# Products of the identity by itself in TensorE's early holes

## The chip, the cores and the metric

One core of one Trainium2 chip runs the whole program as one launch. The metric is the device time in microseconds (us). Five engines are named below: TensorE (PE, with its weight loads as PEld), VectorE (DVE), ScalarE (ACT), GpSimd (POOL) and SyncE (SP), which issues the DMAs.

## The reference

Three blocks follow one another, all in float32:

```python
scores = scale * q @ k.T                                   # 4 batches, 8 heads, 576 x 576, head size 64
scores = where(scores >= max(scores) - tau, scores, -1e9)  # tau = 0.02
attn = exp(scores - max) / (sum + 1e-9);  x = attn @ v     # -> 2304 x 512
g = relu(x @ w_in) ** 2;  y = g @ w_out                    # 512 -> 2048 -> 512
logits = y @ phi                                           # 32 slots: 8 experts of 4
slots = softmax(logits over tokens).T @ y
slots = relu(slots @ w1[e]) @ w2[e]                        # per expert, 512 -> 1024 -> 512
out = softmax(logits over slots) @ slots                   # 2304 x 512
```

## The kernel before, in words

**Front.** `setup()` builds an identity matrix: GpSimd writes it, VectorE copies it to `ident_r` (L280), and `ident` is the same memory read as float32. SyncE then loads five chunks of w_in (128 x 512, `c_load`, L328), the first kt and qt (L536), and goes on with chunks, v, and the kt and qt of later pairs of heads. VectorE and, for every second chunk, ScalarE rework each chunk (`c_low` L344, `c_scale` L338 or L340, the joining `c_shift` L348). For each four chunks TensorE multiplies parts of them by themselves into one PSUM tile (`gram`, `w_gram`, L412: four products a chunk), VectorE takes the diagonal (`w_diag`, L415), TensorE sums it over the partitions (`gtotal`, `w_sum`, L421), and VectorE makes a power-of-two scale from it (`w_scale`, L304 to L306). With that scale ScalarE writes the high half of each chunk (`w_hi`, L437), and the low half is made by VectorE (`w_lo`, L440), by GpSimd (L445, L450) or by TensorE with ScalarE (`w_diff`, L454 and L455).

**Attention.** A tile is 128 queries of a pair of heads. TensorE makes its scores (`s`, L694 and L699) in the only PSUM buffer of that kind. VectorE scales each head and takes its row bound (`top`, L738); when both heads are done, the scores of the next tile may be written. ScalarE takes the exponential (`expo`, L750), VectorE zeroes what lies under the threshold and sums (`keep`, L754), TensorE transposes (`turn`, L275), ScalarE moves the result out of PSUM (`p_evac`, L821), and TensorE multiplies by v. The squares of v are summed for a scale (`v_abs` on ScalarE L559 and L560, `v_sum` on TensorE L564, `v_scale` on VectorE L569).

**The feed-forward block and the end.** From about 140 us on, products of 256 tokens by w_in (L1233), by w_out's precomputed logits, and their transposes run between the attention tiles. The expert block follows from 566 us on: its weights come by DMA while TensorE multiplies them.

**The order.** All of it up to the expert block is put in order by `Plan` while the program is built. Each operation has an engine, a cost, dependencies and a key. The planner keeps a clock of its own and starts on each free engine the ready operation of the lowest key; the order in which it starts them is the order of the instructions on each engine, and nothing on the chip changes it. `HOP` (0.17) is what it adds from one engine to another, `DMA_LEAD` (1.13) and `DMA_TAIL` (0.95) what it adds to a DMA, which holds its model of the bus for 1.46 per chunk and 0.95 per kt or qt. Costs that matter here, in its microseconds: `c_low` 0.35, `c_shift` 0.61, `c_scale` 1.255 on ScalarE and 0.7 on VectorE, `w_gram` 1.1, `s` 1.4, `w_sum` 0.3, `top` 0.813, `v_sum` 0.25, `turn` 0.49, `w_scale` 0.6. TensorE's small results share the tag "mm": four PSUM buffers (`MMB`), taken in rotation, so that the fifth user waits until the first has given its buffer back. A buffer is given back 0.17 after its last reader ends.

Of the kernel before, what the change touches and what calls it, by code (L numbers as in the profile page):

```python
# [36 lines left out]
class Plan:  # L37
# [4 lines left out]
    def __init__(self, caps, shared, wait, ahead):  # L42
        self.shared, self.ops, self.queue = shared, [], {}
        self.caps, self.wait, self.now, self.pending = dict(caps), wait, 0.0, 0
        self.free = {e: 0.0 for e in ENGINES}
        self.cand = {e: [] for e in ENGINES}
        self.gen, self.taken, self.given = {}, {}, {}
        self.times = []
        self.bus, self.ahead = 0.0, ahead
        self.port = 0.0  # L50

    def add(self, eng, cost, fn, deps=(), key=0.0, acq=(), rel=(), dma=0.0, port=False):
# [40 lines left out]
    def start(self, o):  # L93
# [22 lines left out]
        for u in o.users:  # L116
            u.left -= 1
            u.ready = max(u.ready, self.seen(o, u))
            if not u.left:
                self.cand[u.eng].append(u)  # L120

    def run(self, goal=None):
        goal = goal and list(goal)
        if not self.queue:
            for o in sorted(self.ops, key=lambda o: o.key):
                for tag in o.acq:
                    self.queue.setdefault(tag, []).append(o)
        while self.pending:
            if goal is not None:
                goal = [o for o in goal if o.end is None]  # L130
                if not goal:
                    return
            for e in ENGINES:
                if e == "SP" and self.bus - self.now > self.ahead + 1e-6:
                    continue
                if self.free[e] <= self.now + 1e-6:
                    ok = [o for o in self.cand[e] if o.ready <= self.now + self.wait and self.fits(o)]
                    best = min(ok, key=lambda o: o.key, default=None)
                    if best is not None and best.ready <= self.now + 1e-6:
                        self.start(best)  # L140
            while self.times and self.times[0] <= self.now + 1e-6:
                heapq.heappop(self.times)
            assert self.times, "the plan is stuck"
            self.now = heapq.heappop(self.times)
# [3 lines left out]
def tile_kernel(  # L148
# [13 lines left out]
    nc = tc.nc  # L162
# [4 lines left out]
    E, _, F = w1.shape  # L167
    NP = H // 2
    KC = DM // 128
# [44 lines left out]
    QF = 10  # L214
    HDV = (0, 2)
    XHA = ()
    QL = 19.2
    LL = 16.0

# [7 lines left out]
    plan = Plan(  # L227
        dict(
            s=1, ma=1, mm=MMB, old=4, u=UB, e=EB, pt=PTB, rp=3, rb=2, rr=2, hl=HB, vh=1, mx=2, xp=XPB, xh=2, xl=1, gt=MC // 2 + 1,
            gk=GB, l4=1, dT=1, qt=QKB, kt=QKB, vraw=2, vbd=2,  # L230
            sm=5, raw64=RB, cv=CB,
        ),
        ("mm", "ma", "xp", "old"),
        WAIT,
        DQ,
# [6 lines left out]
    def mm_tile(tag="mm"):  # L242
        return psp[tag].tile([128, 512], F32, tag=tag, name="mm")
# [5 lines left out]
    ident = ident_r.bitcast(F32)  # L249
# [27 lines left out]
    def setup():  # L277
        make_identity(nc, sg[:, 0:128])
        nc.vector.memset(ones, 1.0)
        nc.vector.tensor_copy(ident_r, sg[:, 0:128])  # L280
        nc.vector.tensor_scalar(minus, ident, -1.0, None, ALU.mult)
        nc.sync.dma_start(out=tau_sb, in_=tau.partition_broadcast(128))
        nc.vector.tensor_scalar(tau_p, tau_sb, 0.0, None, ALU.max)
        nc.vector.tensor_scalar(nscale, tau_sb, 0.0, -SCALE, ALU.is_ge, ALU.mult)
        nc.vector.tensor_reduce(stack_i, ident.rearrange("p (g s) -> p s g", s=NS), AX.X, ALU.add)
        for g in range(1, NG):
            nc.vector.tensor_copy(stack_f[:, NS * g:NS * g + NS], stack_i)
# [22 lines left out]
    def conv_ops():  # L310
# [82 lines left out]
        def weight_parts(f4):  # L393
            four = range(KC * f4, KC * f4 + KC)
            s2, t, f, inv = [wsc[:, i, f4:f4 + 1] for i in range(4)]
            ws = {}

            def total():
                ws["p"] = mm_tile()
                nc.tensor.matmul(ws["p"][:, 0:KC], ones.to_broadcast([128, 128]), wst[:, four[0]:four[0] + KC], start=True, stop=True)  # L400

            def wscale():
                nc.vector.tensor_reduce(s2, ws["p"][:, 0:KC], AX.X, ALU.add)
                power(s2, t, f, inv)

            def gram():
                ws["g"] = mm_tile()
                for i, n in enumerate(four):
                    y = squared[n][0]["p"].bitcast(BF16)
                    for c in range(0, CW, 128):  # L410
                        z = y[:, 2 * c + 1:2 * c + 256:2]
                        nc.tensor.matmul(ws["g"][:, 0:128], z, z, start=i == 0 and c == 0, stop=i == KC - 1 and c == CW - 128)  # L412

            def diag():
                nc.vector.scalar_tensor_tensor(  # L415
                    ws["g"][:, 0:128], ws["g"][:, 0:128], 1.0, ident, ALU.mult, ALU.mult, accum_out=wst[:, f4:f4 + 1]
                )

            def gtotal():
                ws["p"] = mm_tile()  # L420
                nc.tensor.matmul(ws["p"][:, 0:1], ones.to_broadcast([128, 128]), wst[:, f4:f4 + 1], start=True, stop=True)  # L421

            k = C0 + (four[0] + KC) * TC
            deps = [squared[n][4] for n in four]
            if GRAM:
                gg = add("w_gram", "PE", 1.1, gram, deps, k, ["mm"])
                deps = [add("w_diag", "DVE", 0.3, diag, deps + [gg], k, rel=[("mm", gg)])]
            tt = add("w_sum", "PE", 0.3, gtotal if GRAM else total, deps, k, ["mm"])
            w = add("w_scale", "DVE", 1.0, (lambda: power(ws["p"][:, 0:1], t, f, inv)) if GRAM else wscale, [tt], k, rel=[("mm", tt)])
            wscaled.append(w)  # L430
            scaled = sg[:, f4 * 128:(f4 + 1) * 128]
            wi = add("w_id", "POOL", 0.35, lambda: nc.gpsimd.tensor_scalar(scaled, ident, f, None, ALU.mult), [w], k)
            for n in four:
                o, hi, lo, a, _ = squared[n]

                def high(o=o, hi=hi):
                    nc.scalar.activation(hi, o["p"], AF.Copy, scale=f)  # L437

                def low(o=o, hi=hi, lo=lo):
                    nc.vector.scalar_tensor_tensor(lo, o["p"], f, hi, ALU.mult, ALU.subtract)  # L440

                def times(o=o):
                    for c in range(0, CW, CW // PIECES):
                        i = slice(c, c + CW // PIECES)
                        nc.gpsimd.tensor_tensor(o["p"][:, i], o["p"][:, i], f.to_broadcast([128, CW // PIECES]), ALU.mult)  # L445

                def rest(o=o, hi=hi, lo=lo):
                    for c in range(0, CW, CW // PIECES):
                        i = slice(c, c + CW // PIECES)
                        nc.gpsimd.tensor_tensor(lo[:, i], o["p"][:, i], hi[:, i], ALU.subtract)  # L450

                def diff(o=o, hi=hi):
                    o["pt"] = mm_tile()
                    nc.tensor.matmul(o["pt"], minus, hi, start=True, stop=False)  # L454
                    nc.tensor.matmul(o["pt"], scaled, o["p"], start=False, stop=True)  # L455

                def round_(o=o, lo=lo, n=n):
                    if n % 8 in DIFD:
                        nc.vector.tensor_copy(lo, o["pt"])
                    else:  # L460
                        nc.scalar.activation(lo, o["pt"], AF.Copy)

                k += TC / 4
                h = add("w_hi", "ACT", 0.6, high, [w], k)
                if n % 8 in DIFF:
                    m = add("w_diff", "PE", 1.1, diff, [h, wi], k, ["mm"], [("gt", a)])
                    conv_in.append(add("w_round", "DVE" if n % 8 in DIFD else "ACT", 0.6 if n % 8 in DIFD else 0.51, round_, [m], k, rel=[("mm", m)]))
                elif n % 8 in LOD:
                    conv_in.append(add("w_lo", "DVE", 0.65, low, [h], k, rel=[("gt", a)]))
                else:  # L470
                    m = add("w_times", "POOL", 1.4, times, [h], k)
                    conv_in.append(add("w_rest", "POOL", 1.3, rest, [m], k, rel=[("gt", a)]))
# [11 lines left out]
    def attn_ops():  # L484
# [124 lines left out]
        def split_qk(x):  # L609

            d, k0 = P[x], key(x, -QL)

# [728 lines left out]
    def tail(W, take, ew8, ew6, wr, wx, w8, wg):  # L1341
# [190 lines left out]
        for i in range(B * REM // 128):  # L1532
            ob = row512()
            final(4 * B + i, ob)
            for a in range(2):
                b = 2 * i + a
                nc.sync.dma_start(out=out[b * S + 512:b * S + S, :], in_=ob[64 * a:64 * a + 64])

    setup()
    with tc.manual_schedule():  # L1540
        with ExitStack() as ph:
# [63 lines left out]
```

## Time and profile before

| | |
|---|---|
| time, median of 3 runs | 630.11 us (630.03 to 632.42) |
| profiled execution | 626.73 us, span 624.8 us |
| TensorE busy | 572.7 us, 92% of the span |
| VectorE, ScalarE, GpSimd busy | 448.8 us, 447.9 us, 286.0 us |
| chain that ended last, by engine | TensorE 24%, DMA 6%, VectorE 2%, GpSimd 1% |
| mean granted clock of TensorE | 0.983 |

The span runs from the first to the last instruction; the profiled execution's own time is 1.9 us longer. Busy time is an average over stages: what bounds one stage is read from its own stretch. The records of the granted clock carry a value only from the first change on, so that a clock that is low from the start stands as 1.00 there; the durations of equal instructions tell it.

### The profile page before, as it was taken

How to read it: one execution, taken by the hardware profiler on the slowest of the kernel's cores; microseconds unless marked ns; L12 is line 12 of the kernel's file. 1: busy time of each engine (PE TensorE's matmuls, PEld its weight loads, DVE VectorE, ACT ScalarE, POOL GpSimd, SP SyncE). 2: the span in 40 equal slices, each digit the busy share in tenths (PEclk: the TensorE clock that was granted, in tenths of full speed). 3: DMA queues.
4: the chain of work that ended last, by engine and by line, in shares of the span. 5: the costliest groups of instructions: out<-in, count | busy, mean ns of one | idle time of the engine just before them, and what ended most of it. 6: DMA issues, size and time to landing. Idle time of an engine off the chain costs nothing. (4 is left out here: it accounts for less than half of the span.)

```text
span 624.8 us, 14082 instructions
## 1 busy us (share of the span) xinstructions
PE 572.7 (92%) x5178; PEld 398.8 (64%) x5178; DVE 448.8 (72%) x1265; ACT 447.9 (72%) x848; POOL 286.0 (46%) x464
## 2 busy tenths in 40 slices
PE   3897979989999999999999989999999999999872
PEld 1454546668677678668757756766777877764221
DVE  5799998999988987887888898778762343332233
ACT  2798766678888988988988878988875857441012
POOL 1445672257667766586756658766740000010000
PEclk9999898999999999999999999999999999999997
DMA  8965525677789676585767755554645999999968
GB/s 276 366 215 182 180 83 182 215 181 191 199 149 190 133 175 110 111 177 116 162 138 133 150 105 100 107 107 95 101 77 181 245 345 166 362 355 405 419 256 302
DMA packets 166964, 120.97 MB, mean 194 GB/s; under 512 B 136560, under 2 KB 145520, under 8 KB 164720
## 3 DMA queue, kind: packets, MB, share of 16 engines
q1 hardware_dynamic: 166896, 120.08, 71.5%
q8 instruction: 41, 0.67, 0.4%
q14 instruction: 27, 0.22, 0.1%
HBM read 73.72 MB, written 8.91 MB: 132 GB/s over the span
## 5 line engine op out<-in xcount | busy, mean ns | idle before, releaser
L1233 PEld LDWEIGHTS <-w 128*128 128x128 f16 x1728 | 166.1, 98 | 29.0 <-issue 10.2
L777 POOL TENSOR_TENSOR hl<-e,hl 128x288 f16<-128x288 f32 x192 | 149.2, 801 | 38.0 <-issue 26.8
L1233 PE MATMUL mm<-xh,w 128*128 128x256 f16 x1152 | 149.7, 273 | 0.2 <-ACT gk L1123 0.2
L754 DVE SCALAR_TENSOR_TENSOR e<-u,sm,e 128x576 f32<-128x576 f32 x144 | 121.7, 860 | 18.0 <-ACT e L750 14.3
L750 ACT ACTIVATE e<-u,sm 128x576 f32<-128x576 f32 x144 | 109.2, 771 | 22.3 <-DVE u L738 15.3
L744 POOL TENSOR_SCALAR sm<-sm,tau_p 128x1 f32<-128x1 f32 x144 | 72.4, 508 | 71.3 <-DVE u L738 64.9
L1233 PE MATMUL mm<-xl,w 128*128 128x256 f16 x576 | 86.4, 273 | 0.0
L738 DVE TENSOR_SCALAR_CACHE_REDUCE u<-s,raw 128x576 f32<-128x576 f32 x90 | 71.2, 811 | 13.5 <-PE s L712 12.7
L1243 ACT ACTIVATE gt<-mm,scl 128x512 f32<-128x512 f32 x72 | 49.2, 683 | 43.5 <-PE mm L1233 42.7
L773 ACT ACTIVATE hl<-e 128x576 f16<-128x576 f32 x96 | 64.4, 676 | 2.1 <-DVE e L754 1.5
L841 POOL TENSOR_SCALAR sm<-sm 128x4 f32<-128x4 f32 (+1 forms) x48 | 21.3, 444 | 55.8 <-DVE e L754 47.5
L1251 ACT ACTIVATE gt<-gt 128x512 f32<-128x512 f32 x72 | 45.1, 626 | 1.1
L738 DVE TENSOR_SCALAR_CACHE_REDUCE u<-s,nscale 128x576 f32<-128x576 f32 x54 | 42.6, 807 | 3.2 <-PE s L699 2.7
L1376 POOL MEMSET cv<- 128x512 f32 x4 | 1.9, 524 | 91.6 <-PE mm L1152 91.6
L821 ACT ACTIVATE pt<-mm 128x512 f32<-128x512 f32 x48 | 28.5, 600 | 19.6 <-PE mm L275 19.2
L712 PEld LDWEIGHTS <-qt 128*128 128x128 f16 (+3 forms) x400 | 21.9, 99 | 28.6 <-issue 18.1
L275 PE MATMUL mm<-ident_r,e 128*128 128x128 f32 (+1 forms) x224 | 37.2, 301 | 2.8 <-DVE e L754 2.2
L275 PEld LDWEIGHTS mm<-ident_r,e 128*128 128x128 f32 (+1 forms) x224 | 27.9, 153 | 15.9 <-DVE e L754 5.5
L881 PE MATMUL po<-pt,vh 128*64 128x256 f16 x576 | 36.0, 274 | 0.0
L712 PE MATMUL s<-kt,qt 128*128 128x512 f16 (+1 forms) x200 | 32.9, 289 | 2.4 <-DVE u L738 2.2
L881 PEld LDWEIGHTS <-vh 128*64 128x64 f16 x576 | 29.6, 110 | 5.1 <-issue 4.4
L712 PE MATMUL s<-raw,qt 128*128 128x64 f16 (+1 forms) x200 | 31.2, 293 | 0.0
(205 smaller groups left out, 993.3 us busy)
## 6 DMA issues: line engine op xcount, KB each, us to landing
w<-in_moe_w_dram SPq DMA_DIRECT2D x17, 1024.0 KB, 11.9
w<-in_moe_w_dram SPq DMA_DIRECT2D x26, 512.0 KB, 8.4
raw<-in_moe_w_in_dram SPq DMA_DIRECT2D x16, 511.8 KB, 6.8
raw<-in_moe_w_out_dram SPq DMA_DIRECT2D x16, 511.8 KB, 4.1
raw<-in_v_dram SPq DMA_DIRECT2D x20, 256.0 KB, 3.3
w_out<-cv SPq DMA_DIRECT2D x16, 256.0 KB, 2.7
w<-w_out SPq DMA_DIRECT2D x8, 512.0 KB, 7.4
kt<-in_k_dram SPq DMA_DIRECT2D x10, 320.0 KB, 3.5
```

Of the source, the lines that this page charges most:

```text
L275: nc.tensor.transpose(out_, in_, ident[:n, :n])
L712: nc.tensor.matmul(o0, d["qh"][r, a, q0], kk, start=full, stop=not full)
L738: nc.vector.tensor_scalar(u, o["s"][:, s0:s0 + S], d.get("nscale", nscale), None, ALU.mult, ALU.min, accum_out=gd["sm"][:, c:c + 1])
L744: nc.gpsimd.tensor_scalar(sm[:, 4 + c:5 + c], sm[:, c:c + 1], tau_p, None, ALU.add)
L750: nc.scalar.activation(e, o["u", a], AF.Exp, scale=-1.0, bias=gd["sm"][:, c:c + 1])
L754: nc.vector.scalar_tensor_tensor(e, o["u", a], sm[:, 4 + c:5 + c], e, ALU.is_le, ALU.mult, accum_out=sm[:, 8 + c:9 + c])
L773: nc.scalar.activation(o["hl"][:, a * S:(a + 1) * S], o["e"][:, a * S:(a + 1) * S], AF.Copy)
L777: nc.gpsimd.tensor_tensor(o["hl"][:, 2 * S:][:, i], o["e"][:, i], o["hl"][:, i], ALU.subtract)
L881: nc.tensor.matmul(po[64 * a:64 * a + 64, :n_], d["vh"][:, y, c0:c0 + D], gd["pt"][:, :, c + 5 * a + m, :], start=i == 0 and m == 0, stop= ...
L1233: nc.tensor.matmul(o["h"][:, i * NU:(i + 1) * NU], a, c, start=n_ == 0, stop=n_ == len(terms) - 1)
L1243: nc.scalar.activation(g, o["h"], AF.Relu, scale=down)
L1251: nc.scalar.activation(g, g, AF.Square)
```

## The change

The planner gets a method `idle`. When TensorE has nothing ready and the planner's clock lies between 4.2 and 18.0, it starts one product of the identity by itself (float32, 128 x 128 by 128 x 128) into the next "mm" buffer, booked at 0.43 before 8.0 and at 0.2 from then on. It does so only if that buffer and one more are free and nothing of TensorE becomes ready within half of that cost. Such a product depends on nothing, and its buffer is given back at its end. Besides, for the first four chunks alone, `gram` has four such products behind the first chunk's and four behind the second's, in free columns of its own tile, and `gtotal` four ahead of its sum. The planner's costs of `w_gram` and `w_sum` stay as they were.

```diff
+        self.fill, self.warm = None, (0.0, 0.0, 0.0)
...
+    def idle(self):
+        t0, cold, t1 = self.warm
+        if not t0 <= self.now < t1:
+            return
+        cost = 0.43 if self.now < cold else 0.2
+        n = self.taken.get("mm", 0) + 1
+        if n >= self.caps["mm"] and self.given.get(("mm", self.gen.get("mm", 0), n - self.caps["mm"]), 1e9) > self.now:
+            return
+        if any(o.left == 0 and self.now < o.ready < self.now + cost / 2 for o in self.cand["PE"]):
+            return
+        o = Op("PE", cost, self.fill, 0.0, ("mm",), [], 0.0, False)
+        if not self.fits(o):
+            return
+        self.release(o, [("mm", o)])
+        self.pending += 1
+        self.cand["PE"].append(o)
+        self.start(o)
...
                     if best is not None and best.ready <= self.now + 1e-6:
                         self.start(best)
+                    elif e == "PE":
+                        self.idle()
...
+    GAPS = (4, 4, 0, 0, 4)
+    WARM = (4.2, 8.0, 18.0)
...
                         nc.tensor.matmul(ws["g"][:, 0:128], z, z, start=i == 0 and c == 0, stop=i == KC - 1 and c == CW - 128)
+                    for _ in range(GAPS[i] if f4 == 0 else 0):
+                        nc.tensor.matmul(ws["g"][:, 128:256], ident, ident, start=False, stop=False)
...
                 ws["p"] = mm_tile()
+                for _ in range(GAPS[KC] if f4 == 0 else 0):
+                    nc.tensor.matmul(ws["p"][:, 128:256], ident, ident, start=True, stop=True)
...
+    def filler():
+        nc.tensor.matmul(mm_tile()[:, 0:128], ident, ident, start=True, stop=True)
+
+    plan.fill, plan.warm = filler, WARM
```

## Rows read from the trace of the kernel before

**Rows 1.** The page's 40 slices: the granted clock in tenths of full speed.

```profile
PEclk9999898999999999999999999999999999999997
```

**Rows 2.** Busy time by stage: PE, PEld, DVE, ACT, POOL; then clock, DMA share, GB/s.

```profile
0.00:28.00 28.00, 14.84 (x54) 8.09 (x54) 17.78 (x51) 13.23 (x20) 6.45 (x17) 1.00 0.94 330
28.00:140.00 112.00, 98.22 (x676) 63.29 (x674) 105.36 (x283) 84.24 (x159) 57.35 (x97) 0.94 0.56 177
140.00:470.00 330.00, 322.31 (x3238) 238.69 (x3238) 275.69 (x789) 283.93 (x561) 220.31 (x349) 1.00 0.67 135
470.00:566.00 96.00, 95.73 (x885) 72.04 (x882) 32.79 (x100) 56.46 (x91) 1.92 (x4) 1.00 0.94 281
566.00:605.00 39.00, 34.54 (x303) 12.42 (x304) 10.42 (x32) 4.35 (x8) 0.00 (x0) 1.00 0.98 396
```

**Rows 3.** TensorE in order of time: start, us, line, operation, count, idle before.

```profile
7.55 0.61 PE L412 MATMUL mm<-gt 128*128 128x128 bf16 x4 [7.55 <-DVE gt L348]
...
13.06 0.77 PE L694 MATMUL s<-kt,qt 128*128 128x128 f32 x2 [0.29 <-DMA qt<-in_q_dram]
13.75 2.08 PE L699 MATMUL s<-kt,qt 64*128 64x512 f32 x4
...
17.59 0.76 PE L694 MATMUL s<-kt,qt 128*128 128x128 f32 x2 [1.25 <-DVE u L738]
18.29 2.08 PE L699 MATMUL s<-kt,qt 64*128 64x512 f32 x4
20.30 0.59 PE L564 MATMUL mm<-mx,ones 128*128 128x2 f32 x2
20.74 1.09 PE L275 MATMUL mm<-ident_r,e 128*128 128x128 f32 x4
23.13 0.59 PE L454 MATMUL mm<-w,ctok 128*128 128x512 f16 x1 [1.29 <-ACT w L437]
...
25.22 1.75 PE L275 MATMUL mm<-ident_r,e 128*128 128x128 f32 x9
26.81 0.39 PE L694 MATMUL s<-kt,qt 128*128 128x128 f32 x2
27.13 1.13 PE L699 MATMUL s<-kt,qt 64*128 64x512 f32 x4
28.19 0.76 PE L275 MATMUL mm<-ident_r,e 128*128 128x128 f32 x5
28.79 0.28 PE L564 MATMUL mm<-mx,ones 128*128 128x2 f32 x2
...
35.25 1.09 PE L412 MATMUL mm<-gt 128*128 128x128 bf16 x16
...
61.22 0.76 PE L694 MATMUL s<-kt,qt 128*128 128x128 f32 x2 [3.02 <-issue]
```

**Rows 4.** VectorE in order of time: the identity, joins, `w_scale`'s end, two waits.

```profile
3.79 0.22 DVE L280 CAST ident_r<-sg 128x128 fp32r<-128x128 f32 x1
...
10.65 1.45 DVE L348 SCALAR_TENSOR_TENSOR gt<-raw 128x512 int32<-128x512 int32 x2
...
18.97 0.14 DVE L306 TENSOR_SCALAR wsc<-wsc 128x1 int32<-128x1 int32 x1
...
20.92 0.16 DVE L569 TENSOR_REDUCE mx<-mm 128x1 f32<-128x2 f32 x1 [1.81 <-PE mm L564]
...
28.30 0.82 DVE L738 TENSOR_SCALAR_CACHE_REDUCE u<-s,nscale 128x576 f32<-128x576 f32 x1 [1.30 <-PE s L699]
```

**Rows 5.** ScalarE in order of time: a chunk that waits, the end of `v_abs`.

```profile
15.26 1.34 ACT L340 ACTIVATE raw<-raw 128x512 f16<-128x512 bf16 x1 [3.89 <-DMA raw<-in_moe_w_in_dram]
...
18.24 0.18 ACT L560 ACTIVATION_READ_ACCUMULATOR vh<-vbd 128x1 f32 x1
```

**Rows 6.** Short stretches around a fall and a rise of the granted clock.

```profile
60.50:61.00 0.50, 0.00 (x0) 0.00 (x0) 0.50 (x1) 0.50 (x1) 0.50 (x2) 0.59 0.80 312
...
67.00:67.50 0.50, 0.50 (x2) 0.00 (x0) 0.12 (x2) 0.35 (x1) 0.50 (x3) 0.58 0.00 0
```

## The prediction

> **What bounds the kernel now.** I read the windows by stage first, for who is the bottleneck when. Until 28 us no engine is: VectorE is busy for 17.78 of 28.00, TensorE for 14.84, while the DMA share is 0.94. From 28 to 140 VectorE is, with 105.36 of 112.00; from 140 to 470 TensorE, with 322.31 of 330.00, and to 566 with 95.73 of 96.00; from 566 to 605 the DMA, at 0.98 [rows 2]. A gain at the front that reaches VectorE by 28 us is therefore handed on, from one saturated resource to the next, if nothing with a time of its own stands between.
>
> Second, the front's TensorE in order of time. The granted clock shows 9 in the first slices [rows 1], but equal instructions say otherwise: the scores of a tile last from 13.06 to 13.75+2.08=15.83 and from 17.59 to 20.37, 2.77 us each, but the next take 1.45 (26.81 to 27.13+1.13=28.26) [rows 3]. So TensorE runs at 1.2 GHz until the nine transposes at 25.22, which straddle the change: it rises near 25.9. Before that it had worked nearly without a stop from 23.13, 2.8 us; it had not risen over the busy stretch from 17.59 to 21.83 [rows 3]. At the other rise, near 67.3, it had been busy since 61.22, 6.1 us [rows 3, 6].
>
> Third, the waits in the front. Does VectorE wait for slow TensorE work? Twice: 1.81 us before 20.92 for `v_sum`, which stands behind the second tile's scores, and 1.30 us before 28.30 for the third tile's scores [rows 4].
>
> **The change part by part.** *How many products.* From the planner's costs: the fourth chunk arrives on its clock at 1.13+4x1.46+0.95+0.17=8.09; head 1.255, hop 0.17, join 0.61, hop 0.17 put `w_gram` at 10.295. The hole from 4.23 to there takes 9 products at 0.43 (to 8.10) and 11 at 0.2 (to 10.30). `w_sum` ends at 13.15, the second `s` starts at 15.06; here only two fit, because `w_sum` holds its buffer until `w_scale` has ended. They push `turn` one round further: it now needs the buffer of `w_sum`, free at 17.09, and slips from 16.71 to 17.09, to 17.58 at its end. Two more fit behind it. That is 24, and with 12 in `gram` and `gtotal` 36 products, two MATMULs each if they are issued as L694 is.
>
> *Price of one.* Not in the trace as such; the nearest rows bound it. Dear ends: L694, one float32 product of this shape, takes 0.69 to the next start when slow (13.06 to 13.75) and 0.32 when fast (26.81 to 27.13), with a weight load exposed that a run of equal products needn't show. Cheap ends, from runs of float32 operations with the identity, two for one product: nine in 1.59 (25.22 to 26.81, partly fast) give 0.36 slow, five in 0.60 (28.19 to 28.79) give 0.24 fast; the four in 1.09 at 20.74, all at 1.2 GHz, give 0.54 [rows 3]. I take 0.44 slow, between the two runs, and 0.24 fast, since a run of products is what stands here.
>
> *The clock's rise.* The identity is written at 4.01 [rows 4], so the products start near 4.1. With 2.8 to 6.1 us of work before a rise, as at the two rises, it comes between 6.9 and 10.2; I take 8.6. Then 10 products are at 1.2 GHz, 10 at 2.4: 4.1+4.4+2.4=10.9 (7 at 1.2: 10.3; 14: 11.7).
>
> The Trainium skill ("TensorE: Matmul & The Clock Gate", Part 1) warns that the number of products at the low clock at a start differs, 6, 11 or 14 for one kernel, and advises against fitting to a count; here the count is fixed when the program is built. By it, 6 to 14 of them move the end of the 20 by 8x0.20=1.6 us, an estimate; one execution, as in the trace of before, cannot show it.
>
> *What stands behind them.* `gram`, which ran piece by piece as chunks came (7.55 on), now waits for all 20. Its MATMULs are 0.07 each when fast (16 in 1.09): two chunks at 0.27, eight products at 0.24, two more chunks: 3.0 us, ending at 13.9 (13.3 to 14.7), where the fourth chunk's join at 12.10 is no longer last [rows 3, 4]. The first scores wait for qt until 13.06 anyway; they now run from 13.9 to 15.4 (14.8 to 16.2) instead of 15.83. So far 0.4 gained, or as little as -0.4: the products ahead eat most of the first tile's gain. At the dear ends (6 at 0.69, 14 at 0.32, then eight at 0.32) these scores would end at 18.0, 2.1 late.
>
> *Second tile.* From the end of the first scores to the second's start lie the two `top`s, 1.76 us (15.83 to 17.59). TensorE's new work there, 4x0.24 + 0.3 + 2x0.24=1.7, just fits under it; at half speed it would not, by some 1.4 us. Second scores: 17.2 to 18.6 instead of 20.37, 1.75 gained. `v_sum` also needs `v_abs`, which ends at 18.42 and doesn't move: ScalarE sits behind a chunk that lands at 15.26 by DMA, in a stretch where the DMA share is 0.94 [rows 2, 5]. So `v_sum` moves from 20.30 to 18.65 (18.45 to 19.45) and takes 0.28 for 0.59 [rows 3]: VectorE's wait at 20.92 ends 1.95 us earlier (1.2 to 2.2, and at the dear ends not at all). `turn` behind it has the added wait for `w_scale`, which ended at 19.11 [rows 4] and comes no later now, when `v_sum` ends: it hides there, and queued behind it is only `w_diff`.
>
> *To 28 us.* TensorE saves about 0.5 on the four transposes, 1.1 on `w_diff` (23.13 to 25.22, halved) and 0.5 on the nine transposes [rows 3], which takes the third scores out of VectorE's way: of the 1.30 before 28.30 [rows 4] I count 0.75, since ScalarE's and GpSimd's steps between stay as long as they were; ends 0 and 1.30. Late next is VectorE's own work. Sum: 1.95+0.75=2.7 us; ends 0 (dear products) and 3.5. The transfers behind it have room: the DMA share is 0.56 from 28 us on [rows 2].
>
> The profiled execution would go from 626.73 (span 624.8 and 1.93 around it) to 624.0. It lies 3.4 below the median of the runs; against that median, 630.11, I forecast 627.4.
>
> **The rivals.** *Order, for the worse (slower).* The slip of `turn` is not a delay alone: at 17.70 ScalarE finds it not ready and takes a second `w_hi` ahead of `p_evac`. From there the planner chooses on another clock, and the order of all later work is another. Its place is 28 to 140, where VectorE has 6.64 us of idle time and TensorE 13.78 [rows 2]. TensorE stood still for 3.02 us before 61.22, the clock fell at 60.7 and came back at 67.3: 6.6 us at half speed, up to 3.3 lost [rows 3, 6]. One more such hole cancels the 2.7; from the second on it is slower: 2x3.3-2.7=+3.9, 634.0. For it: nothing in an order chosen on a model of the time guards against such holes. Against it: VectorE's work is the same and 94% dense.
>
> *Order, for the better.* The same, with that hole closed: 2.7+3.3=6.0, 624.1.
>
> *Absorbed.* The front is earlier, but something with its own time takes it back: the tail from 566, at a DMA share of 0.98, would start no sooner if its weights had been held back by the DMA and not by buffers. 630.1. Against it: from 470 to 566 TensorE is 99.7% busy, and loads wait for buffers that it frees.
>
> *The clock doesn't rise.* The busy stretch from 17.59 to 21.83 didn't raise it, and the 20 products need not either. All slow: 4.1+8.8=12.9, `gram` with 8x0.44 and 2.4 of its own (four MATMULs in 0.61 [rows 3]) to 18.8, first scores to 21.6, 5.8 late; then 4x0.44+0.6+2x0.44=3.2 instead of 1.76, 7.3 late: 637.4. Against it: 8.8 us without a hole is longer than either stretch that ended in a rise.
>
> **How the numbers follow.** Forecast 0.42 (own range 625.9 to 628.9), order for the better 0.18, absorbed 0.17, order for the worse 0.17 (630.5 to 635), no rise 0.06. A measurement of this kernel tells 0.5%, 3.15 us, from no change: below 626.96 or above 633.26. Faster: 0.42x0.42 of the forecast and all of the better order, 0.36. Slower: half of the worse order and no rise, 0.15. Same: 0.49. Range 622.5 to 633.0: about 0.04 lies below and 0.15 above.
>
> **What would show it.** Right: products from 4.1 on, first at 0.44, then 0.24; no 2.08 in L699 before 28 us; first scores ending at 15.4, second at 18.6, `v_sum` at 18.65; VectorE's waits of 1.81 and 1.30 gone or short; stage 28 to 140 as long as before, its end near 137. Wrong: L699 still at 2.08 in the second tile; `gram` ending after 14.7; another count than 20 products ahead of it; or the front earlier and the end not, with new falls of the granted clock before 140.

## The result, and the profile after

The change makes the kernel slower: 634.83 us (median of 13 runs) against 628.04 us of 13 runs of the kernel before beside them, ratio 1.0085 (95% interval 1.0062 to 1.0108). The ratio is the recorded one; the quotient of the two medians is 1.0108. All ratios leave out runs over 1.5% above the fastest of their kernel, which are two of the four of p2 below and no others, so that p2's median stands higher than its ratio. The forecast was 627.4, faster, in a range of 622.5 to 633.0. The profiled execution took 632.96 us, its span 631.1.

What I had forecast for TensorE's front came, within 0.2 us. TensorE of the changed kernel, in order of time (start, us, line, operation, count, idle before), as in [rows 3]; lines from L298 on are those of before plus 23 to 27:

```profile
4.07 7.04 PE L1567 MATMUL mm<-ident_r 128*128 128x128 f32 x40 [4.07 <-DVE ident_r L303]
10.95 0.39 PE L435 MATMUL mm<-gt 128*128 128x128 bf16 x4
11.18 1.11 PE L437 MATMUL mm<-ident_r 128*128 128x128 f32 x8
...
13.76 0.44 PE L721 MATMUL s<-kt,qt 128*128 128x128 f32 x2
14.12 1.13 PE L726 MATMUL s<-kt,qt 64*128 64x512 f32 x4
...
16.32 0.69 PE L1567 MATMUL mm<-ident_r 128*128 128x128 f32 x4
17.27 0.46 PE L721 MATMUL s<-kt,qt 128*128 128x128 f32 x2 [0.26 <-DVE u L765]
17.65 1.13 PE L726 MATMUL s<-kt,qt 64*128 64x512 f32 x4
18.71 0.38 PE L591 MATMUL mm<-mx,ones 128*128 128x2 f32 x2
...
21.76 0.47 PE L721 MATMUL s<-kt,qt 128*128 128x128 f32 x2
```

The 20 products end at 10.95 (forecast 10.9), the second scores at 18.8 (18.6), `v_sum` starts at 18.71 (18.65), and no scores take 2.08 any more: at 2.4 GHz they take 1.13. VectorE's waits of 1.81 and 1.30 [rows 4] are 0.35 and none (the last line is of e1, an experiment below that keeps the order of before):

```profile
19.13 0.16 DVE L596 TENSOR_REDUCE mx<-mm 128x1 f32<-128x2 f32 x1 [0.35 <-PE mm L591]
...
24.11 0.81 DVE L765 TENSOR_SCALAR_CACHE_REDUCE u<-s,nscale 128x576 f32<-128x576 f32 x1
```

```profile
24.38 0.79 DVE L765 TENSOR_SCALAR_CACHE_REDUCE u<-s,nscale 128x576 f32<-128x576 f32 x1
```

The third tile's row bound starts at 24.11 instead of 28.30. So 4.2 us are won by 28 us, more than the 2.7 that I had counted (part of it because the new order puts other work of VectorE behind this bound; with the order of before it starts at 24.38, 3.9 earlier), and the span ends 6.3 later. The windows by stage, as in [rows 2], show where TensorE waits more: between 140 and 470 it is idle for 330.00-317.66=12.3 us, before for 7.7.

```profile
0.00:28.00 28.00, 22.56 (x147) 17.53 (x149) 20.98 (x58) 16.64 (x30) 10.44 (x21) 1.00 0.95 329
28.00:140.00 112.00, 99.10 (x712) 66.30 (x709) 107.73 (x290) 85.67 (x157) 59.60 (x96) 0.97 0.61 200
140.00:470.00 330.00, 317.66 (x3149) 232.48 (x3148) 265.33 (x768) 276.06 (x549) 213.42 (x342) 0.99 0.63 126
470.00:566.00 96.00, 95.52 (x891) 72.33 (x891) 34.31 (x105) 56.73 (x91) 3.90 (x7) 1.00 0.93 264
566.00:605.00 39.00, 35.23 (x281) 12.70 (x278) 8.76 (x30) 3.95 (x8) 0.00 (x0) 1.00 1.02 403
```

Which date carries that to the end? SyncE's queue, the last products with v and the last feed-forward products, first of the kernel before, then of the changed one (start, us, operation, count):

```profile
440.80 29.30 SPq L784 DMA_TRANSPOSE pt<-hl  x5
477.32 1.30 SPq L1301 DMA_DIRECT2D w<-in_moe_w_dram  x3
...
476.23 0.50 PE L886 MATMUL po<-pt,vh 128*128 128x256 f16 x3
...
549.55 0.60 PE L1233 MATMUL mm<-xl,w 128*128 128x256 f16 x4
```

```profile
439.87 34.84 SPq L811 DMA_TRANSPOSE pt<-hl  x6
483.90 0.35 SPq L1328 DMA_DIRECT2D w<-in_moe_w_dram  x1
...
482.81 0.50 PE L913 MATMUL po<-pt,vh 128*128 128x256 f16 x3
...
552.49 0.60 PE L1260 MATMUL mm<-xl,w 128*128 128x256 f16 x4
```

The last products with v end at 476.73 before and at 483.31 after; half a microsecond later the first expert weights are asked for, into the memory that attention frees. From that issue to the end of the span it is 147.5 us before and 147.2 after. TensorE's own feed-forward products end at 550.15 and 553.09, only 2.9 apart. So attention ends 6.6 us later, and the end follows it. The order in which the planner put the work is another from the slip of `turn` on, as the prediction had seen. ScalarE before, then after:

```profile
19.09 0.72 ACT L437 ACTIVATE w<-gt,wsc 128x512 f16<-128x512 f32 x1
21.87 0.60 ACT L821 ACTIVATE pt<-mm 128x512 f32<-128x512 f32 x1 [2.07 <-PE mm L275]
22.37 0.71 ACT L437 ACTIVATE w<-gt,wsc 128x512 f16<-128x512 f32 x1
```

```profile
18.76 1.33 ACT L464 ACTIVATE w<-gt,wsc 128x512 f16<-128x512 f32 x2
20.00 0.57 ACT L848 ACTIVATE pt<-mm 128x512 f32<-128x512 f32 x1
```

Two `w_hi` now stand ahead of the first `p_evac`.

### The profile page after: what moved, and what is told of

Same layout as the page of the kernel before. It is cut to its first block, busy times and chain, and to the rows that moved or that the text cites. A ratio compares the mean times of both kernels' runs of the same rounds, so it can differ in the third digit from the quotient of the medians.

```text
span 631.1 us, 14203 instructions
## 1 busy us (share of the span) xinstructions
PE 582.4 (92%) x5250; PEld 407.8 (65%) x5250; DVE 446.5 (71%) x1265; ACT 446.0 (71%) x848; POOL 287.4 (46%) x464
## 4 chain that ended last, share of the span: by engine, by line
PE 58%; DVE 17%; DMA 10%; ACT 6%; POOL 3%; issue 3%; SPq 1%; DVEq 0%; ACTq 0%; POOLq 0%
PE mm L1260 28%; PE mm L298 6%; DMA w<-in_moe_w_dram 6%; PE s L739 6%; PE po L908 5%; DVE e L781 4%; DVE u L765 4%; DMA raw<-in_moe_w_in_dram 2%; PE mm L1179 2%; PE mm L1014 2%; PE po L900 2%; DMA w<-w_out 2%; PE po L913 1%; ACT e L777 1%; PE mm L402 1%
## 5 line engine op out<-in xcount | busy, mean ns | idle before, releaser
L804 POOL TENSOR_TENSOR hl<-e,hl 128x288 f16<-128x288 f32 x192 | 153.0, 820 | 43.0 <-issue 26.0
L781 DVE SCALAR_TENSOR_TENSOR e<-u,sm,e 128x576 f32<-128x576 f32 x144 | 125.3, 884 | 19.7 <-ACT e L777 15.5
L765 DVE TENSOR_SCALAR_CACHE_REDUCE u<-s,raw 128x576 f32<-128x576 f32 x90 | 71.6, 811 | 10.2 <-PE s L739 9.4
L298 PE MATMUL mm<-ident_r,e 128*128 128x128 f32 (+1 forms) x224 | 35.5, 286 | 7.3 <-DVE e L781 7.1
L868 POOL TENSOR_SCALAR sm<-sm 128x4 f32<-128x4 f32 (+1 forms) x48 | 17.8, 370 | 53.1 <-DVE e L781 40.6
L298 PEld LDWEIGHTS mm<-ident_r,e 128*128 128x128 f32 (+1 forms) x224 | 25.1, 142 | 21.2 <-DVE e L781 8.2
L363 ACT ACTIVATE raw<-raw 128x512 f16<-128x512 bf16 x16 | 21.8, 1363 | 13.3 <-DMA raw<-in_moe_w_in_dram 12.5
```

The costliest lines, as they stand in the source:

```text
L298: nc.tensor.transpose(out_, in_, ident[:n, :n])
L765: nc.vector.tensor_scalar(u, o["s"][:, s0:s0 + S], d.get("nscale", nscale), None, ALU.mult, ALU.min, accum_out=gd["sm"][:, c:c + 1])
L781: nc.vector.scalar_tensor_tensor(e, o["u", a], sm[:, 4 + c:5 + c], e, ALU.is_le, ALU.mult, accum_out=sm[:, 8 + c:9 + c])
L804: nc.gpsimd.tensor_tensor(o["hl"][:, 2 * S:][:, i], o["e"][:, i], o["hl"][:, i], ALU.subtract)
```

## The experiments

Eleven runs, each beside runs of the kernel before on the same chip; the ratio is to those, not to the first line of the table. "First load" is the issue of the first expert weights in the profiled execution, "rest" the span less that.

| run | median us | ratio (95%) | first load | span | rest |
|---|---|---|---|---|---|
| before | 628.04 | | 477.32 | 624.8 | 147.5 |
| changed | 634.83 | 1.0085 (1.0062 to 1.0108) | 483.90 | 631.1 | 147.2 |
| e1_order_kept | 628.19 | 0.9994 (0.9965 to 1.0022) | 479.67 | 627.1 | 147.4 |
| e1b_order_kept | 628.00 | 0.9979 (0.9949 to 1.0009) | 482.37 | 629.5 | 147.1 |
| e2_one_more | 636.30 | 1.0114 (1.0079 to 1.0149) | 485.69 | 633.1 | 147.4 |
| e3_order_alone | 638.22 | 1.0140 (1.0111 to 1.0169) | 489.00 | 636.4 | 147.4 |
| e4_late_weights | 633.81 | 1.0080 (1.0043 to 1.0117) | 478.34 | 631.8 | 153.5 |
| e6_hold_136 | 626.25 | 0.9949 (0.9926 to 0.9973) | 477.65 | 624.2 | 146.6 |
| e7_hold_three | 623.74 | 0.9919 (0.9891 to 0.9948) | 473.44 | 621.1 | 147.7 |
| e8_hold_no_front | 626.74 | 0.9948 (0.9921 to 0.9976) | 478.94 | 627.1 | 148.2 |
| p1_hop | 639.13 | 1.0133 (1.0068 to 1.0197) | 493.18 | 639.9 | 146.7 |
| p2_top | 645.91 | 1.0168 (1.0075 to 1.0261) | 494.22 | 641.8 | 147.6 |
| p3_low | 639.66 | 1.0148 (1.0087 to 1.0210) | 493.00 | 640.3 | 147.3 |

**Is it the order or the products?** The window of the change is closed earlier, so that one product fits behind `w_sum` (e1), or two (e2); with one, the planner starts everything as in the kernel before.

```diff
-    WARM = (4.2, 8.0, 18.0)
+    WARM = (4.2, 8.0, 13.3)     # e1 and e1b: 21 products
+    WARM = (4.2, 8.0, 13.4)     # e2: 22 products
```

> The changed kernel with the planner's window for products closed at 13.3 instead of 18.0: 21 products instead of 24 (one instead of two behind the sum), and the 12 in the Gram product and ahead of its sum as before. With one product there, the planner starts every operation in the order of the kernel before. Theory A, the new order is what costs: with the old order the early gain survives; second scores end near 18.7, attention ends and the first expert weight load is issued some 3 us ahead of the 477.3 of the kernel before, near 474; time 3 us less, ratio 0.995 (0.991 to 0.998). Theory B, the products themselves cost later (a clock, a buffer, an engine): ratio 1.000 or above, weight load at 477 or later.

> The same with the window closed at 13.4: 22 products, one more than in the run with 13.3. The second product behind the sum takes one more buffer of the rotation, the planner's transposes slip by 0.39, and its order from there on is that of the changed kernel. Theory A: as slow as the changed kernel, ratio 1.008 (1.005 to 1.012), first expert weight load near 484. Theory B: one product of 0.2 us more than the run with 13.3, so the same time as that within 0.1%.

One product of 0.22 us lies between 0.9994 and 1.0114. In the traces every engine of e1 has its instructions in the order of the kernel before, and in e2 in that of the changed kernel. The order costs, and the products don't: theory A. Nor is it the clock in these traces: between 28 us and the end of attention it was low for 20.5 us in e1 and for 13.7 in the slower e2. But e1 missed its 0.995: the early gain isn't in its time.

The other side, the new order without any product:

```diff
-    GAPS = (4, 4, 0, 0, 4)
+    GAPS = (0, 0, 0, 0, 0)
...
     def filler():
-        nc.tensor.matmul(mm_tile()[:, 0:128], ident, ident, start=True, stop=True)
+        pass
```

> The changed kernel's planner and order, with none of the products issued: neither the 24 in the holes nor the 12 others. Theory A: the new order without the early clock, so slower than the changed kernel by the early gain of about 3 us: ratio 1.013 (1.008 to 1.017), first expert weight load near 487. Theory B: as fast as the kernel before, 1.000, because what costs is gone.

It is 1.0140 and its weights come 5.1 us after the changed kernel's: the order alone loses more, and in that order the products win something back. (Its clock was low for 23.9 us between 28 and the end of attention, the changed kernel's for 13.7.)

**Does the end of attention set the end?**

```diff
-        for n, f in enumerate([ew8] * 9 + [ew6]):
-            add("w_load", "SP", 0.5, f, [], n - 100, dma=2.6 if f is ew8 else 1.3)
+        spare = dram.tile([640, F], F32, name="spare")
+
+        def held():
+            for i in range(2):
+                nc.sync.dma_start(out=spare[i * 320:i * 320 + 320, :], in_=w1[i, 0:320, :])
+            ew8()
+
+        for n, f in enumerate([ew8, held] + [ew8] * 7 + [ew6]):
+            add("w_load", "SP", 0.5, f, [], n - 100, dma=1.3 if f is ew6 else 2.6)
```

> The kernel before with two copies of 1.31 MB inside DRAM put between the first and the second expert weight load; nothing else moves. Theory C, from the end of attention on the stream of weight loads sets the end: 2.62 MB at the 0.40 MB per us that this stretch moves is 6.5 us, and the time grows by about that, ratio 1.010 (1.006 to 1.020, a copy inside DRAM may take longer per byte than a load). Rival D, TensorE's products of the feed-forward block, which end near 550, set the end and the weights have slack: within 0.2% of the kernel before.

Its rest is 153.5, 6.0 above 147.5, and the ratio 1.0080, as theory C has it. But this run alone doesn't tell C from D: the copies also held up the two transposes behind them on SyncE's queue (14.42 us from the start of the first to the end of the second, for 8.29 before), TensorE stood idle for 2.6 us, its clock fell, and its feed-forward products ended at 557.7 instead of 550.2. TensorE of e4 in that stretch:

```profile
500.00:510.00 10.00, 7.38 (x36) 4.44 (x34) 5.25 (x18) 3.26 (x7) 0.00 (x0) 0.72 1.05 256
```

What tells them apart are the other twelve traces, without the copies. Their spans, from 621.1 to 641.8, have a rest between 146.6 and 148.2. From the last feed-forward product to the end it is 73.8 to 75.3 us in the order of before, but 77.0 to 78.4 in the others. And from the issue of the last weight load to the end it is 33.0 to 33.1 in all thirteen. So it is the weights that carry the date, theory C.

**Where did e1's early gain go?** Its trace is about 3 us ahead of that of the kernel before until 138 us and 2.2 behind from 148 on, with the same order of instructions. TensorE of e1:

```profile
134.25 1.08 PE L402 MATMUL mm<-l,gk 128*128 128x32 f32 x8
136.89 0.46 PE L721 MATMUL s<-kt,qt 128*128 128x128 f32 x2 [1.56 <-DVE rp L873]
137.28 1.48 PE L726 MATMUL s<-kt,qt 64*128 64x512 f32 x4
138.69 5.33 PE L402 MATMUL mm<-l,gk 128*128 128x32 f32 x24
```

and of the kernel before:

```profile
137.65 0.98 PE L379 MATMUL mm<-l,gk 128*128 128x32 f32 x8
139.57 0.46 PE L694 MATMUL s<-kt,qt 128*128 128x128 f32 x2 [0.93 <-DVE rp L846]
139.96 1.13 PE L699 MATMUL s<-kt,qt 64*128 64x512 f32 x4
141.02 2.87 PE L379 MATMUL mm<-l,gk 128*128 128x32 f32 x24
```

The same 24 products take 5.33 instead of 2.87: the clock fell, at 137.9, after the hole of 1.56. The granted clock of e1 near there (PE, PEld, DVE, ACT, POOL busy; clock, DMA share, GB/s):

```profile
137.00:138.00 1.00, 1.00 (x6) 0.46 (x6) 1.00 (x3) 1.00 (x3) 1.00 (x3) 0.97 1.02 381
138.00:139.00 1.00, 1.00 (x4) 0.32 (x2) 1.00 (x3) 1.00 (x3) 1.00 (x1) 0.50 0.68 256
...
146.00:147.00 1.00, 1.00 (x6) 0.81 (x5) 1.00 (x3) 0.00 (x0) 0.00 (x0) 0.50 1.02 373
```

So products go into the holes before such falls, in free columns of tiles that are TensorE's anyway; the planner doesn't see them.

```diff
                         start=kk == 0, stop=kk == KC - 1,
                     )
+                for _ in range(6 if m == 5 else 0):           # e6, e7, e8: hole before 136.89
+                    nc.tensor.matmul(o["pt"][:, 128:256], ident, ident, start=True, stop=True)
...
                 nc.tensor.matmul(ws["p"][:, 0:1], ones.to_broadcast([128, 128]), wst[:, f4:f4 + 1], start=True, stop=True)
+                for _ in range(12 if f4 == 2 else 0):         # e7, e8: hole before 57.9
+                    nc.tensor.matmul(ws["p"][:, 128:256], ident, ident, start=True, stop=True)
...
                             nc.tensor.matmul(po[i, :n_], lt, rh, start=m == 0, stop=m == 4)
+                    for _ in range(6 if p == 4 and g == 2 else 0):   # e7, e8: hole before 87.1
+                        nc.tensor.matmul(po[:, 256:384], ident, ident, start=True, stop=True)
```

e6 and e7 build on e1, e8 on the kernel before.

> The run with the old order and 21 early products, with 6 more products behind the logit products of w_out's sixth chunk, in free columns of their tile: TensorE then works through 5/6 of its hole before 136.89, after which the clock fell for some 8 us in that run while it had not in the kernel before. The planner doesn't know of them. Theory F, the early gain of 3.2 us was there until 141 and this one fall took 5.4 back: without it the first expert weight load comes near 474.5 and the time is 3 us below the kernel before, ratio 0.995 (0.990 to 0.998). Rival G, a transfer or another engine with a time of its own holds the work there, and the low clock beside it costs nothing: weight load at 479 to 480, ratio 0.999 to 1.001.

> The same with products in two more holes after which the clock fell in the kernel before as well: 12 behind the third group's partition sum (hole of 3.0 us before 57.9) and 6 behind the first product with v of the last 64 tokens (hole of 1.6 us before 87.1). Theory F: the clock stays up from 10 to 150 or falls later and shorter, and each fall saved is worth 2 to 4 us: weight load near 470, ratio 0.990 (0.985 to 0.996). Rival G: VectorE bounds this stretch and a slow TensorE is hidden behind it: the same as without these 18, 0.995.

> The kernel before with the 24 products in the three later holes alone, none before 28 us and nothing changed in the planner. Theory F: the falls after 60.7 and 91 are spared, ratio 0.994 (0.988 to 1.000), about 3 us above the run with both. Rival G: 1.000.

> The run with the old order and 21 early products once more, for a second trace. Theory F: where the clock falls after the hole before 136.9 the weight load is near 479.7, and where it doesn't it is near 474.5; ratio between 0.994 and 1.002. Rival G: weight load near 479.7 with or without a fall.

The times are as theory F has them, in all three: 0.9949, 0.9919, 0.9948. The mean granted clocks of all runs go with them: 0.977 in e1b, 0.980 in e6, 0.988 in e7, 0.990 in e8 and 0.980 in the 35 runs of the kernel before beside them; among these 35 a run is 4.3 us shorter for each 0.01 more of clock (correlation -0.79). e6 is 2.2 us below e1b (0.7 to 3.8, means of 12 runs each), and its six products are the only difference.

The single traces are less tidy. In e1b the clock fell at 140.0, after the same hole of 1.56, and in both e1 and e1b it stayed low for 10.2 us. In e6, with that hole filled, this fall is gone, but a shorter one stands ahead of it, at 132.8 for 3.4 us, and its weights came at 477.65, not near 474.5; that execution (626.21) is at the median of its runs, while the kernel before was profiled in 626.73, below the 629.79 of the runs beside e6. e8 was profiled in 629.05, its slowest run, and e4, which has the instructions of the kernel before up to 478 us, shows a fall at 135.7 that the kernel before doesn't. So a profile of one execution doesn't show which falls a kernel has. In e7 only one fall is left, 3.4 us from 128.8. Its windows, and those of e1 for the same stretches:

```profile
50.00:60.00 10.00, 9.39 (x58) 6.19 (x54) 9.03 (x20) 8.79 (x16) 7.56 (x11) 1.00 0.35 115
60.00:70.00 10.00, 8.86 (x63) 5.48 (x63) 9.89 (x23) 5.83 (x12) 6.87 (x10) 1.00 0.45 136
85.00:100.00 15.00, 12.95 (x101) 8.42 (x100) 14.87 (x40) 8.14 (x16) 5.53 (x9) 1.00 0.47 137
140.00:150.00 10.00, 10.00 (x91) 7.60 (x89) 9.21 (x25) 8.46 (x18) 6.83 (x12) 1.00 0.73 195
```

```profile
50.00:60.00 10.00, 6.32 (x30) 3.43 (x30) 9.03 (x20) 8.80 (x16) 7.77 (x11) 0.97 0.38 114
60.00:70.00 10.00, 9.58 (x43) 5.60 (x44) 8.70 (x21) 4.93 (x9) 6.21 (x9) 0.69 0.38 127
85.00:100.00 15.00, 11.57 (x76) 7.39 (x70) 13.62 (x37) 6.88 (x15) 6.50 (x11) 0.89 0.40 132
140.00:150.00 10.00, 10.00 (x51) 7.91 (x51) 6.80 (x17) 3.49 (x7) 3.88 (x9) 0.59 0.70 192
```

Where TensorE stays at 2.4 GHz, VectorE is busier in three of the four stretches (9.89 against 8.70, 14.87 against 13.62, 9.21 against 6.80): in these two traces it is the bound only while TensorE keeps up. e7 is faster than both kernels, by 0.81% (0.52 to 1.09) than the one before. And e7 against e8 is the early products alone, in the order of before and with the later holes filled: 2.2 us (0.7 to 3.7, means of 12 runs each) of the 2.7 forecast.

**Is it this reordering, or any?** Three kernels without a product, in which one number of the planner is moved by 0.001 (p2 and p3: one entry of a long line of costs):

```diff
-HOP = 0.17
+HOP = 0.171                      # p1
...
-('top', 'DVE'): 0.813
+('top', 'DVE'): 0.812            # p2
-('low', 'POOL'): 0.695
+('low', 'POOL'): 0.696           # p3
```

> The kernel before, with no product anywhere, and the planner's time between two engines set to 0.171 instead of 0.170. Every instruction stays; the order is another from some early tie on. Theory H, the order of the kernel before is a chosen one among many and any shift of the planner's clock draws another, mostly worse: 0.7 to 1.6% slower, ratio 1.011, first expert weight load 5 to 11 us later than 477.3. Rival I, the loss belongs to the slip of the transposes behind the sum and another shift costs nothing: ratio 0.997 to 1.003.

> The same with the planner's cost of VectorE's row bound set to 0.812 instead of 0.813 and nothing else. Theory H: 0.7 to 1.6% slower, ratio 1.011. Rival I: 0.997 to 1.003.

> The same with the planner's cost of GpSimd's low half set to 0.696 instead of 0.695 and nothing else. Theory H: 0.4 to 1.4% slower, ratio 1.008. Rival I: 0.997 to 1.003.

All three are slower, by 1.3 to 1.7%, with weights 15.7 to 16.9 us later in their traces: theory H, beyond its sizes but for the time of p1. Part of that can be the clock, which was low for 27.3, 34.1 and 23.9 us between 28 us and the end of attention, against 13.7 in the kernel before. Of the five orders measured here, that of the kernel before is the fastest.

## Why the prediction was wrong

*Right:* 24 products and their places; the price of a MATMUL, 0.213 and 0.111 us by the starts in a row, 0.43 and 0.22 for a product (taken: 0.44 and 0.24); the rise of the clock at 8.9 (taken: 8.6, between 6.9 and 10.2); `gram`, both scores, `v_sum`; the slip of `turn` and ScalarE's choice behind it. VectorE's second wait vanished whole instead of by 0.75, and with it a wait of 0.37 for GpSimd before 23.84, so the gain by 28 us was 3.9 with the order kept (e1), and 4.2 in the changed kernel, instead of 2.7.

*The step that failed:* "A gain at the front that reaches VectorE by 28 us is therefore handed on, from one saturated resource to the next". It presumes the order of before. With that order and the later holes filled, 2.2 us were handed on (e7 against e8); in the new order the front's gain came, and attention still ended 6.6 us late. I had the reordering among the rivals, with 0.17 for the worse, and held better and worse to be about even; p1 to p3 and e3 say that another order costs 1.3 to 1.7%. The diff showed that the change runs through the planner, and the kernel that its costs are given to three digits; the chance of a worse order had to be most of it.

*Also wrong in that rival:* its mechanism. I priced it by more falls of the clock, one at 3.3 us. The changed kernel's clock was low for 13.7 us between 28 us and the end of attention, and for 13.7 before. That the measured 634.83 lies in its 630.5 to 635 is luck. What the new order did was to bring attention's end late: 24 more of the feed-forward products by w_in (1200 against 1176) and 8 more of the logits' (96 against 88) stand ahead of attention's last product, some 3.6 us of work (0.11 and 0.125 each), and from 28 us to there TensorE is idle for 25.45 us against 21.47. The stretch from 140 to there, before and changed:

```profile
140.00:476.73 336.73, 329.04 (x3309) 243.61 (x3312) 276.44 (x790) 288.29 (x568) 220.31 (x349) 1.00 0.66 134
```

```profile
140.00:483.31 343.31, 330.76 (x3284) 242.16 (x3284) 269.51 (x778) 283.29 (x562) 215.41 (x344) 0.99 0.63 124
```

*And a limit that I had read as harmless:* the weights' transfers from 470 on [rows 2]. I had them wait for buffers that TensorE frees. Some of the later ones do (14.4 us in the kernel before), but the first ones start when attention's memory goes, the DMA share of the kernel before is 0.86 or more in every ten microseconds from 480 to 600, and the end comes 147 us after that start, whether 552 of the products by w_in are still to come then or 528. So what is moved ahead of attention's end is paid there.

*Handed on, with the order kept?* Only in part. The price of a fall was about right, half its length (5.5 us for 10.2 in e1, 1.9 for 3.4 in e6); its place was not: a front that is 3 us earlier met a hole of 1.56 instead of 0.93, the clock fell, and the same kernel ended at 0.9994 (e1) and 0.9979 (e1b). That it loses by this fall is shown by e6 in the times, not in the one trace; why the hole is wider there is not shown.

*Slips in its readings.* The clock of the kernel before rose at 26.5 and not near 25.9: at the prices since measured, the nine transposes in 1.59 us [rows 3] are nearly six slow ones and three fast. It fell at 60.6 and came back at 67.4 [rows 6], 6.8 us instead of 6.6. The first scores at the dear ends come to 17.8 instead of 18.0. And the estimate of 1.6 us for 6 to 14 products is 0.8 if these are MATMULs, of which a product has two. None of this decides anything.

The number of products at the low clock differs between executions: of the first 40 MATMULs about 18 ran at it in e1 and 27 in e1b, which is the same kernel, and 22 and 27 in the changed kernel and e2; that is 9, 13.5, 11 and 13.5 products. From e1 to e1b it moved the end of the 20 from 10.62 to 11.64. The warning of the Trainium skill ("TensorE: Matmul & The Clock Gate", Part 1), that the point of the rise moves from run to run and that one shouldn't fit to a count, agrees with these numbers.

Where the new order's attention falls back can be told: against the kernel before, the same product with v is 3.9 us early in the changed kernel at 238.5, and 6.6 late at 332.5. In e2, whose clock is at 2.4 GHz throughout that stretch, it goes from 0.5 early to 8.4 late. The stretch of the kernel before, then that of e2:

```profile
238.53:332.50 93.97, 91.43 (x941) 66.34 (x941) 77.61 (x225) 84.11 (x169) 61.82 (x101) 1.00 0.68 136
```

```profile
238.05:340.91 102.86, 96.88 (x981) 69.36 (x981) 86.67 (x236) 86.78 (x174) 68.77 (x106) 1.00 0.69 141
```

Every engine has more to do there, VectorE 9 us more, and TensorE is idle for 6.0 us against 2.5. What stays open is why the planner's order puts that work there, and why the traces of p1 to p3 come later than e3's.

## What to carry to other kernels

Where a planner with tuned costs orders the work, an edit that touches the planner's clock is two edits, the one meant and a new order; build the effect outside the planner, or compare against the same order, before crediting or blaming it. Look for the date from which the last saturated stage counts (here the end of attention, 147 us ahead of the end): a gain that doesn't move that date is no gain. Products that keep the clock up belong in the holes ahead of a fall, where TensorE would stand idle: 24 of them, at 0.22 us each, in three such holes made the kernel before 0.5% faster (e8).

## What the runs showed of the hardware

A fall of the clock isn't a property of the kernel alone: e1 and e1b are the same kernel, and the clock fell at 90.2 for 3.4 us in the one and at 88.8 for 6.8 us in the other. In p2, which has no products in the front, the clock had risen by 23.39 (scores in 1.13 at 25.86), while in the kernel before it rose at 26.5. And with holes as short as 1.6 us before 87 and 1.7 before 89.5 it fell at 90.2 in the trace of e1; with 6 products in the first of the two it stayed up in that of e7.
